# Attention and ResMLP on one core: alpha2 folded into w_ch1 once, beta2 turned into a relu bias, and the instruction order refined anew

## The chip, the cores and the metric

The kernel runs on one core of one Trainium2 chip. The metric is the device time of one execution in microseconds. The core has five engines that each run their own instruction list in order: TensorE (PE, matrix products; its weight loads are listed apart as PEld), VectorE (DVE), ScalarE (ACT), GpSimd (POOL) and SyncE (SP, which here issues most of the DMA transfers). "SPq" in a profile is SP's list, where DMA issues and their waits stand. POOL also issues some transfers; the profile calls their queue software_dynamic and the others' hardware_dynamic.

## The reference

```python
# attention, B=4, H=8, S=768, D=64; 4 sinks and a causal window of 128
scores = (q @ k.T) / sqrt(D), kept where (key is a sink) or (0 <= i - j < 128)
a = softmax(scores);  x = a @ v              # -> x: (4, 768, 512)

# ResMLP
a1  = alpha1 * x + beta1
tok = einsum('ts,bsd->btd', w_tok, a1)       # mixing over the 768 tokens
u   = x + lam * tok
a2  = alpha2 * u + beta2                     # per channel, 512 of them
ch  = relu(a2 @ w_ch1) @ w_ch2               # 512 -> 2048 -> 512
out = u + lam * ch
```

All inputs and the output are float32.

## The kernel before, in words

The four batches go through the same steps: load q, k and v, transpose q and k, scores (S), exponentials (E), masks, the product with v (pv), token mixing (tok), transposed u (uT), the first channel product (h), relu into hT, and the second channel product. Matrix operands are f16, sums are f32.

**The plan.** Each step is put down as a task: a priority, the engines that may run it with a cost in ns for each, the tasks that it needs, and the buffers that it uses. `Plan.run` (L132) lays all the tasks out against a model of the engines and the DMA queues, and `Plan.emit` (L246) writes the instructions out in that order. On the chip each engine works through its own list in order and waits by semaphores for the data that the tasks name. A DMA "lands" in the plan at a modelled time; a dependence on it holds in the plan, but if the two are not connected by data, nothing on the chip enforces it. The list `TURNS` holds seeds that perturb the priorities. In the first 36 us of the plan, where PE has nothing to do, fillers are emitted (`idle`, L347 to L349): small matmuls on a constant tile `warm`, 75 ns each by the plan.

**Weights.** `load_w1` (L553 to L558) brings w_ch1 into `w1f` (f16, 128 x 4 x 2048) as four quarters of 512 columns, converted on the way by POOL's software queue. `load_w` (L548) brings w_ch2 in eight pieces of 512 KB into f32 staging tiles `wst`; the plan has them follow the second quarter of w1f. `cast_w2` (L933 to L939) multiplies them by lam into `w2f`. `gate` (L560 to L564) is a tiny transfer on SP that reads one value row of a w1f quarter into a scratch tile: it must wait for the quarter to land, and every transfer that stands behind it on SP's list waits with it. There are three gates, for the quarters 1, 2 and 3.

**uT.** u = x + lam·tok is cast to f16. For batch 0, `uTp` (L985) transposes on PE into PSUM, and four pieces per half of the tokens evacuate it with alpha2·u + beta2 applied (`affine`, L977 to L983, on ACT at L980 or on DVE at L982, both factors as per-partition pointers). For batches 1 to 3, `uTx` (L1009 to L1026) lets a DMA transpose on SP write uT directly, and eight affine pieces per batch (128 x 384 each, ACT or DVE, in place) follow.

**The channel MLP.** `mlp1` (L1028 to L1049): for each half of the tokens (384) and each of the 16 blocks of 128 hidden channels, four matmuls over the 512 channels into one PSUM bank (tile `h`, L1036), then relu into `hT` on ACT (L1042) or DVE (L1044). That is 32 groups of four matmuls for each batch. Groups are called h0_0_10 for batch 0, half 0, hidden block 10; block i reads quarter i // 4 of w1f. The second product is plain for batch 0 (`mlp2`, tile `ch`, L1221). For batches 1 to 3 it is a Strassen scheme of seven products (`prod`, P1 to P7, L1153), which needs sums of hT parts (`h_sums`: S3 L1094, S1 L1095, S2 L1096, S4 L1097) and of w2f parts (`w2_sums`, L1057 to L1068).

Batch b+1's attention is woven into batch b's MLP, so PE's list mixes both.

The four h matmuls of a group and the affine piece are these lines:

```python
nc.tensor.matmul(ph.t, w1f[:, c, fi * P : (fi + 1) * P],
                 bu.t[:, c, chk * NTOK : (chk + 1) * NTOK], start=(c == 0), stop=(c == NC - 1))
nc.scalar.activation(o, i, AF.Identity, bias=be, scale=al)       # affine on ACT
```

Of the kernel before, what the change touches and what calls it, by code (L numbers as in the profile page):

```python
# [9 lines left out]
FP32 = mybir.dt.float32  # L10
# [101 lines left out]
class Plan:  # L112
# [18 lines left out]

    def run(self, prio):  # L132

# [34 lines left out]
        def pick():  # L168
            best = None
            spare = {k: sorted(h for h, x in zip(homes[k], busy[k]) if not x) for k in homes}  # L170
            for r, i in open_:
                at = ready[i]
                if best is not None and at > best[0]:
                    continue
                t = tasks[i]
                asked = {}
                for b in t.uses:
                    if b.home is None:
                        asked[b.kind] = asked.get(b.kind, 0) + 1
                if any(len(spare[k]) < n for k, n in asked.items()):  # L180
                    continue
                at = max([at] + [spare[k][n - 1] for k, n in asked.items()])
                own = None
                for e in t.engs:
                    at_e = max(free[e], at)
                    if e == POOL or (e == DVE and t.port):
                        at_e = max(at_e, port)
                    key = (at_e + FW * t.engs[e], at_e, r, at_e + t.engs[e], i, e)
                    if own is None or key < own:
                        own = key  # L190
                if best is None or own[1:] < best:
                    best = own[1:]
            return best
# [51 lines left out]

    def emit(self, turns):  # L246

        prio = [t.prio for t in self.tasks]
        for seed in turns:
            prio = shuffle(prio, seed)  # L250
        for t, e, start, stop, idle in self.run(prio):
            t.at = (e, start, stop)
            if idle:
                self.fill[1](self.pools["d"][0].tile(
                    [128, 512], FP32, tag=f"d_{idle[0]}", bufs=1, name=f"idle{t.i}"), idle[1])
            for b in t.uses:
                if b.t is None:
                    pool, shape, dtype = self.pools[b.kind]
                    b.t = pool.tile(b.shape or shape, b.dtype or dtype,
                                    tag=f"{b.kind}_{b.home}", bufs=1, name=b.name)  # L260
            t.fn(e)


# [16 lines left out]
def kernel(  # L280
# [52 lines left out]
        "u16": (sb, [P, DM], FP16),  # L333
        "uT": (sb, [P, NC, S], FP16),
        "hT": (sb, [P, NF, NTOK], FP16),
        "wst": (sb, [P, 2, 512], FP32),
# [30 lines left out]

    rsum = const.tile([P, NR], FP32, name="rsum")
    ab_row = sb.tile([2 * NC, P], FP32, tag="pt_2", bufs=1, name="ab_row")
    nc.scalar.dma_start(ab_row[0:NC], moe_alpha2.rearrange("(c p) -> c p", p=P))  # L370
# [37 lines left out]

    gates = sb.tile([1, 32], FP16, tag="pt_1", bufs=1, name="gates")

# [5 lines left out]

    TURNS = (13523, 134113, 50022, 128275, 136711, 187603, 125671, 100730, 14946, 163131, 178432, 158827, 183776, 137680, 153375, 26742, 367527, 307353, 376563, 212018, 255075, 397706, 218147, 375675, 393913, 224567, 207692, 352780, 243076, 346008)
    W1_SINCE = 20000.0
# [271 lines left out]
    def scores(p, b, j, Gs, bias=False):  # L690
# [51 lines left out]
        for G, hps, n, pS, eT in units:  # L742
            done["S", b, j, G] = a

            def ex(e, n=n, pS=pS, eT=eT):
                nc.scalar.activation(  # L746
                    eT.t, pS.t[:, :, 0 : n * w].rearrange("p e (i w) -> p e i w", i=n),
                    AF.Exp, scale=scale)

            x_ = add(p + 0.1, {ACT: 170 + 2 * n * w * 0.835}, ex, [a], [pS, eT])  # L750
            if not bias:
                def mk(e, eT=eT):
                    if e == POOL:
                        ev = eT.t.rearrange("p e i w -> p (e i) w")
                        keep(ev[:, :, 0:P], 0, 1, -1)
                        if w > P:
                            keep(ev[:, :, P:w], -1, -1, 1)
                        return
                    m = mask0 if j == 0 else (maskn if j < NR - 1 else maskn[:, :, 0:P])
                    ev = eT.t.rearrange("p e i w -> p (e i) w")  # L760
                    nc.vector.tensor_mul(ev, ev, m.to_broadcast(list(ev.shape)))

                c = {DVE: 60 + 2 * n * w * 0.66}
                if b and j:
                    c[POOL] = 2 * (150 + n * w * 0.9)
                x_ = add(p + 0.2, c, mk, [x_], [eT], port=True)
            for g in (0, 1) if G is None else (G,):
                off = 2 * g if G is None else 0
                E[b, j, g] = (eT, off)
                done["E", b, j, g] = [x_]  # L770
# [38 lines left out]
    def pv(p, b, r, G):  # L809
# [55 lines left out]
        elif G == 1:  # L865
# [7 lines left out]

            a = add(p + 0.3, {POOL: 1350}, mul, [a, done["x", b, r, 0], done["la1"]], [bx, bt], port=True)
            done["xh", b, r, 1] = add(
# [57 lines left out]
    def cast_w2(p, i):  # L933
        for a in range(4 * i, 4 * i + 4):
            src = wst[f"w2_{a - a % 2}"]
            done["w2", a] = add(
                p, {DVE: 980, POOL: 1400},
                lambda e, a=a, src=src: engine[e].tensor_mul(w2f[:, a, :], src.t[:, a % 2, :], lam_b),
# [70 lines left out]
    def uTx(p, b, ti):  # L1009

        if (b, 0) not in uT:
            uT[b, 0] = Buf("uT", None, None, f"uT{b}")
        bo, bu = uT[b, 0], u16[b, ti]
        done["uTd", b, ti] = add(
            p, {SP: 1220}, lambda e: nc.sync.dma_start_transpose(
                bo.t[:, :, ti * P : (ti + 1) * P], bu.t),
            [done["u16", b, ti]], [bu, bo], lands=(6, 100))
        if ti % 3 < 2:
            return
        chk = ti // 3  # L1020
        for c in range(NC):
            o = (c, slice(chk * NTOK, (chk + 1) * NTOK))
            done["uT", b, chk, c] = add(
                p + 0.1 + 0.01 * c, {DVE: 380, ACT: 700},
                lambda e, c=c, o=o: affine(e, bo.t[:, o[0], o[1]], bo.t[:, o[0], o[1]], c),
                [done["uTd", b, 3 * chk + i] for i in range(3)] + [done["ab2"]], [bo])  # L1026

    def mlp1(p, b, chk, fi):  # L1028
        if fi == 0:
            hT[b, chk] = Buf("hT", None, None, f"hT{b}_{chk}")  # L1030
        bh, bu = hT[b, chk], uT[b, 0]
        ph = Buf("d", [P, NTOK], FP32, f"h{b}_{chk}_{fi}")

        def mm(e):
            for c in range(NC):
                nc.tensor.matmul(  # L1036
                    ph.t, w1f[:, c, fi * P : (fi + 1) * P],
                    bu.t[:, c, chk * NTOK : (chk + 1) * NTOK], start=(c == 0), stop=(c == NC - 1))

        def relu(e):  # L1040
            if e == ACT:
                nc.scalar.activation(bh.t[:, fi, :], ph.t, AF.Relu)  # L1042
            else:
                nc.vector.tensor_scalar_max(bh.t[:, fi, :], ph.t, 0.0)  # L1044

        a = add(p, {PE: 4 * 161}, mm,
                [done["uT", b, chk, c] for c in range(NC)] + [done["w1", fi // 4]],
                [ph, bu])
        done["h", b, chk, fi] = add(p + 0.1, {ACT: 493, DVE: 556}, relu, [a], [ph, bh])  # L1049

# [6 lines left out]
    def w2_sums(p):  # L1057

        for g in range(HF // 2):
# [5 lines left out]
            def sub(o, i0, i1, after, n_):  # L1065
                def f_(e, bw=bw):
                    ab = [w2f[:, x_[0], x_[1]] if isinstance(x_, tuple) else bw.t[:, x_] for x_ in (o, i0, i1)]
                    engine[e].tensor_sub(*ab)  # L1068
                return add(p + 4 * g + n_, {DVE: 420, POOL: 1400}, f_, after, [bw], port=True)

# [7 lines left out]
    def h_sums(p, b, what):  # L1078
# [6 lines left out]
        def s2(g, f):  # L1085
            return own[g].t if own else h0.t[:, f]

        if what == "S3":
            hs = hS[b] = [Buf("nat", [P, HF // 2, NTOK], FP16, f"hS{b}_{g}") for g in range(2)]
        for g in range(2):  # L1090
            f, k_ = slice(4 * g, 4 * g + 4), slice(HF + 4 * g, HF + 4 * g + 4)
            fi, ki = range(4 * g, 4 * g + 4), range(HF + 4 * g, HF + 4 * g + 4)
            made = {
                "S3": lambda e, f=f, g=g: nc.vector.tensor_sub(hs[g].t, h0.t[:, f], h1.t[:, f]),  # L1094
                "S1": lambda e, f=f, k_=k_: nc.vector.tensor_add(h1.t[:, f], h1.t[:, f], h1.t[:, k_]),  # L1095
                "S2": lambda e, f=f, g=g: nc.vector.tensor_sub(s2(g, f), h1.t[:, f], h0.t[:, f]),  # L1096
                "S4": lambda e, f=f, k_=k_, g=g: nc.vector.tensor_sub(h0.t[:, k_], h0.t[:, k_], s2(g, f)),  # L1097
            }[what]
# [10 lines left out]
            uses = uses + ([own[g]] if own and what in ("S2", "S4") else [])  # L1109
            done[what, b, g] = add(p + 0.1 * g, {DVE: 880}, made, after, uses, port=True)  # L1110

# [5 lines left out]
    def prod(p, b, what, nt):  # L1117
# [46 lines left out]
        def plus(p, bx, cols, more):  # L1164
            def f_(e):
                nc.vector.tensor_add(row(bx)[:, cols], row(bx)[:, cols], pc.t)  # L1166
            u_ = done["u16", b, nt if bx is top else nt + 3]
            return add(p, {DVE: 400}, f_, [a, u_] + more, [pc, bx])

# [12 lines left out]
        elif what == "P6":  # L1182
            def u2(e):
                nc.vector.tensor_add(bt.t, bt.t, pc.t)

            u = add(p + 0.1, {DVE: 400}, u2, [a, done["read", b, "P1", nt]], [pc, bt])

# [7 lines left out]

            done["U12", b, nt] = add(p + 0.3, {POOL: 760, DVE: 400}, ot, [u, done["u16", b, nt]], [bt, top], port=True)
            done["U2", b, nt] = add(
# [108 lines left out]
    for b in range(B):  # L1306
# [54 lines left out]
        if b + 1 == STRASSEN[0]:  # L1361
            w2_sums(w0 + ns + PAR["w2s"])
        if b + 1 < B:
            nb = b + 1
# [28 lines left out]

    plan.emit(TURNS)

# [34 lines left out]
```

The softmax here doesn't subtract the row's maximum and nothing guards it: scores larger than these inputs give would overflow.

## Time and profile before

| | |
|---|---|
| device time, median of 5 runs | 256.57 us (256.34 to 257.22) |
| the profiled execution's own time | 256.68 us |
| its span, first to last instruction | 255.0 us |
| mean granted TensorE clock | 1.00 |
| busy: PE / DVE / ACT / POOL | 247.6 / 189.2 / 142.6 / 88.1 us |
| bytes moved by DMA | 38.80 MB, 152 GB/s in the mean |

A line of groups has the source line, engine and operation, `out<-in` by tile names, partitions x elements and type, the count, then total busy time and mean ns of one, then the idle time of that engine just ahead of such instructions and what ended it. A line of waits has the waiting engine and line, what it waited for, and the total, the number and the longest of these waits in us. A timeline line has the start, the length, and what ran.

By stage of the kernel, PE and ACT were busy for:

| stretch, us | PE busy | DVE busy | ACT busy | POOL busy | DMA share |
|---|---|---|---|---|---|
| 0 to 40 | 38.13 | 31.50 | 26.42 | 21.05 | 1.07 |
| 40 to 64 | 23.54 | 17.78 | 21.05 | 9.67 | 1.05 |
| 64 to 104 | 38.83 | 32.80 | 19.54 | 14.99 | 0.86 |
| 104 to 130 | 25.92 | 20.28 | 22.70 | 15.65 | 0.86 |
| 130 to 180 | 49.64 | 41.04 | 25.32 | 21.75 | 0.59 |
| 180 to 252 | 71.58 | 45.73 | 27.58 | 5.02 | 0.19 |

### The profile page before, as it was taken

The numbers are of one execution on the slowest core, as the hardware profiler recorded it, in microseconds if no ns is written. First come the engines' busy times: TensorE is split into PE (matmuls) and PEld (weight loads), VectorE is DVE, ScalarE is ACT, GpSimd is POOL, SyncE is SP. The second block draws the span as 40 slices with busy tenths as digits, with TensorE's granted clock in tenths as the row PEclk, the third lists the DMA queues.
The fourth block names the chain that finished last, engine by engine and source line by source line (L and its number), as shares of the span: only waits on it lengthen the run. The fifth ranks groups of instructions, "written<-read, shape, count | busy, mean of one in ns | idle before, by whom it ended". The sixth has DMA issues, their size and how long they took to land.

```text
span 255.0 us, 5519 instructions
## 1 busy us (share of the span) xinstructions
PE 247.6 (97%) x2174; PEld 161.4 (63%) x2174; DVE 189.2 (74%) x402; ACT 142.6 (56%) x236; POOL 88.1 (35%) x108
## 2 busy tenths in 40 slices
PE   8999998999999999899999999999999999999994
PEld 7855645665555543456688676658658666657883
DVE  6787998595878878578889988877789764136782
ACT  2699846989848035688971225867571135775000
POOL 7419802345455330168653450735310101000000
PEclk9999999999999999999999999999999999999999
DMA  6999999999944899599679699501000257000105
GB/s 206 200 219 320 205 252 389 376 354 192 219 74 119 185 245 209 113 207 228 145 144 194 108 194 249 85 3 21 3 0 3 61 167 144 0 0 3 63 4 185
DMA packets 86130, 38.80 MB, mean 152 GB/s; under 512 B 73540, under 2 KB 80460, under 8 KB 86104
## 3 DMA queue, kind: packets, MB, share of 16 engines
q1 hardware_dynamic: 82320, 35.14, 57.7%
q0 software_dynamic: 3744, 3.28, 8.0%
q8 instruction: 17, 0.28, 0.5%
q14 instruction: 9, 0.07, 0.1%
q10 hardware_dynamic: 40, 0.03, 0.0%
HBM read 29.91 MB, written 6.29 MB: 142 GB/s over the span
## 4 chain that ended last, share of the span: by engine, by line
PE 92%; DVE 3%; DMA 2%; ACT 1%; issue 1%; ACTq 0%
PE h L1036 33%; PE P L1153 21%; PE tok L956 11%; PE ch L1221 8%; PE pv L825 5%; PE S L724 4%; PE idle L349 2%; PE S L719 1%; PE tp L614 1%; DMA wtn<-in_moe_w_tok_dram 1%; DVE uT L982 1%; PE tp L611 1%; PE pv L818 1%; PE wT L916 1%; PE sk L656 1%; ACT uT L980 1%
## 5 line engine op out<-in xcount | busy, mean ns | idle before, releaser
L1036 PE MATMUL h<-uT,w1f 128*128 128x384 f16 x512 | 92.0, 326 | 2.7 <-DVE uT L982 1.3
L1036 PEld LDWEIGHTS <-w1f 128*128 128x128 f16 x512 | 47.3, 98 | 34.4 <-issue 5.5
L1042 ACT ACTIVATE hT<-h 128x384 f16<-128x384 f32 x99 | 48.4, 493 | 25.9 <-PE h L1036 25.5
L1153 PEld LDWEIGHTS <-hT 128*128 128x128 f16 x408 | 39.8, 98 | 6.7
L746 ACT ACTIVATE E<-S 128x1024 f16<-128x1024 f32 (+1 forms) x39 | 37.9, 1001 | 7.5 <-PE S L724 3.7
L869 POOL TENSOR_TENSOR tm<-x,la_b 128x512 f32<-128x512 f32 x18 | 26.2, 1455 | 26.3 <-DVE xh L872 19.1
L956 PE MATMUL tok<-xh,wtokT 128*128 128x512 f16 x144 | 33.4, 379 | 0.0
L356 ACT CAST u<-x 128x512 f16<-128x512 f32 x19 | 11.7, 618 | 30.7 <-DVE x L963 30.5
L1153 PE MATMUL P<-w2f,hT 128*128 128x256 f16 x216 | 25.9, 273 | 0.0
L1044 DVE TENSOR_SCALAR hT<-h 128x384 f16<-128x384 f32 x29 | 15.8, 552 | 11.6 <-PE h L1036 11.2
L1166 DVE TENSOR_TENSOR x<-x,P 128x256 f32<-128x256 f32 x45 | 18.3, 417 | 8.2 <-PE P L1153 8.0
L956 PEld LDWEIGHTS <-wtokT 128*128 128x128 f16 x144 | 14.0, 98 | 14.6
L1221 PE MATMUL ch<-w2f,hT 128*128 128x512 f16 x96 | 23.0, 379 | 0.0
L1153 PE MATMUL P<-w2s,hT 128*128 128x256 f16 x192 | 22.8, 273 | 0.0
L851 DVE TENSOR_TENSOR x<-pv,rec 128x256 f32<-128x256 f32 x48 | 20.4, 424 | 1.7
L358 POOL CAST vfs<-vnat 128x512 f16<-128x512 f32 x18 | 14.9, 834 | 16.2 <-DMA vnat<-in_v_dram 16.0
L963 DVE TENSOR_TENSOR x<-x,tok 128x512 f32<-128x512 f32 x24 | 16.2, 683 | 5.7 <-PE tok L956 5.7
L356 ACT CAST n<-nat 128x768 f16<-128x768 f32 x16 | 13.2, 829 | 11.4 <-DMA nat<-in_q_dram 8.5
L825 PEld LDWEIGHTS <-E 128*128 128x128 f16 x328 | 15.2, 98 | 6.0 <-issue 1.6
L825 PE MATMUL pv<-vfs,E 128*128 128x65 f16 x328 | 17.9, 194 | 0.0
L358 POOL CAST u<-x 128x512 f16<-128x512 f32 x5 | 3.1, 623 | 34.2 <-DVE x L963 21.1
L1221 PEld LDWEIGHTS <-hT 128*128 128x128 f16 x96 | 8.6, 98 | 9.0 <-issue 0.2
(131 smaller groups left out, 327.5 us busy)
## 6 DMA issues: line engine op xcount, KB each, us to landing
out_dram<-x SPq DMA_DIRECT2D x21, 256.0 KB, 2.8
nat<-in_q_dram SPq DMA_DIRECT2D x13, 384.0 KB, 5.8
nat<-in_k_dram SPq DMA_DIRECT2D x13, 384.0 KB, 5.5
vnat<-in_v_dram SPq DMA_DIRECT2D x18, 256.0 KB, 4.4
wst_w<-in_moe_w_ch_dram SPq DMA_DIRECT2D x8, 512.0 KB, 7.5
wtn<-in_moe_w_tok_dram SPq DMA_DIRECT2D x6, 384.0 KB, 4.2
w1f<-in_moe_w_ch_dram POOLq DMA_DIRECT2D x4, 512.0 KB, 10.2
v<-in_v_dram SPq DMA_DIRECT2D x12, 128.0 KB, 6.0
```

The source lines that it names most:

```text
L356: nc.scalar.copy(o, i)
L358: engine[e].tensor_copy(o, i)
L746: nc.scalar.activation(eT.t, pS.t[:, :, 0 : n * w].rearrange("p e (i w) -> p e i w", i=n), AF.Exp, scale=scale)
L825: nc.tensor.matmul(po.t[:, hl, :], eT.t[:, e_, off + i, c : c + P], vf[j][:, h, :], start=(r < 2 and n == 0), stop=(n == len(parts) - 1 an ...
L851: nc.vector.tensor_mul(bx.t[:, 4 * G : 4 * G + 4, :], po.t[:, :, 0:D], rec.t.to_broadcast([P, 4, D]))
L869: engine[e].tensor_mul(bt.t, bx.t.rearrange("p h d -> p (h d)"), la1_b)
L956: nc.tensor.matmul(pt.t, wtokT[:, si, ti * P : (ti + 1) * P], hs[si].t, start=(si == 0), stop=(si == NR - 1))
L1036: nc.tensor.matmul(ph.t, w1f[:, c, fi * P : (fi + 1) * P], bu.t[:, c, chk * NTOK : (chk + 1) * NTOK], start=(c == 0), stop=(c == NC - 1))
L1042: nc.scalar.activation(bh.t[:, fi, :], ph.t, AF.Relu)
L1153: nc.tensor.matmul(pc.t, hh[:, nt * P : (nt + 1) * P], w(fi), start=(first and n_ == 0), stop=(n_ == HF - 1), skip_group_check=True)
L1166: nc.vector.tensor_add(row(bx)[:, cols], row(bx)[:, cols], pc.t)
L1221: nc.tensor.matmul(pc.t, bh.t[:, fi, nt * P : (nt + 1) * P], w2f[:, fi, :], start=(fi == 0), stop=(fi == NF - 1))
```

## The change

Since a2 @ w_ch1 = u @ (alpha2·w_ch1) + beta2 @ w_ch1, alpha2 can be multiplied into w_ch1's rows and beta2 @ w_ch1 added ahead of the relu.

- Batch 0 stays as it was, on the plain w1f, with two more columns: columns 768 and 769 of its uT hold +beta2 and −beta2 (`beta_cols`, 2 small DVE instructions). The second half's 16 groups are 386 columns wide. After the relu their difference is beta2 @ w_ch1 exactly, relu(z) − relu(−z) = z; one subtraction puts it into `bw1` (128 x 16, f32).
- Once batch 0's h groups have read w1f, `fold_w1` multiplies it in place by alpha2, in eight pieces of 128 x 1024.
- Batches 1 to 3 have no affine pieces. h needs the DMA transposes and the folds, and the relu gets `bw1`'s column as a per-partition bias.
- The buffers uT and hT are wider (784 and 386 columns), and the h sums read 384 of 386. The scratch tile of the gates has a place of its own.
- Some costs in the plan differ, `TURNS` has 16 seeds in place of 30, and a list `NUDGES` of several hundred seeds moves priorities of single tasks, groups of them or pairs, or pins a task to one of its engines. The order of all engines' lists is thereby another one.

```diff
@@ uTx: batches 1 to 3
-        done["uTd", b, ti] = add(
+        done["uT", b, ti] = add(
             p, {SP: 1220}, lambda e: nc.sync.dma_start_transpose(
                 bo.t[:, :, ti * P : (ti + 1) * P], bu.t),
             [done["u16", b, ti]], [bu, bo], lands=(6, 100))
-        if ti % 3 < 2:
-            return
-        chk = ti // 3
-        for c in range(NC):
-            o = (c, slice(chk * NTOK, (chk + 1) * NTOK))
-            done["uT", b, chk, c] = add(
-                p + 0.1 + 0.01 * c, {DVE: 380, ACT: 700},
-                lambda e, c=c, o=o: affine(e, bo.t[:, o[0], o[1]], bo.t[:, o[0], o[1]], c),
-                [done["uTd", b, 3 * chk + i] for i in range(3)] + [done["ab2"]], [bo])
+    def beta_cols(p):
...
+                nc.vector.tensor_scalar(
+                    out=bo.t[:, :, S + n_], in0=beta2_c, scalar1=sign, scalar2=None, op0=ALU.mult)
...
+    def fold_w1(p):
...
+            lambda e: engine[e].tensor_sub(bw1, bh.t[:, :, NTOK], bh.t[:, :, NTOK + 1]),
+            [done["h", 0, 1, fi] for fi in range(NF)], [bh])
+        for fh in range(2):
+            for c in range(NC):
+                o = (c, slice(fh * DFF // 2, (fh + 1) * DFF // 2))
+                def fold(e, o=o):
+                    w, al = w1f[:, o[0], o[1]], alpha2_c[:, o[0] : o[0] + 1]
+                    if e == ACT:
+                        nc.scalar.activation(w, w, AF.Copy, scale=al)
+                    else:
+                        engine[e].tensor_scalar(out=w, in0=w, scalar1=al, scalar2=None, op0=ALU.mult)
+                done["w1a", c, fh] = add(
+                    p + 0.1 * (4 * fh + c), {ACT: 1060, DVE: 650}, fold,
+                    [done["hm", 0, chk, fi] for chk in range(2) for fi in range(8 * fh, 8 * fh + 8)]
+                    + [done["ab2"]], port=True)
@@ mlp1
         def relu(e):
+            o, be = bh.t[:, fi, 0:n_], bw1[:, fi : fi + 1]
             if e == ACT:
-                nc.scalar.activation(bh.t[:, fi, :], ph.t, AF.Relu)
+                nc.scalar.activation(o, ph.t, AF.Relu, **({"bias": be} if b else {}))
+            elif b:
+                nc.vector.tensor_scalar(out=o, in0=ph.t, scalar1=be, scalar2=0.0, op0=ALU.add, op1=ALU.max)
             else:
-                nc.vector.tensor_scalar_max(bh.t[:, fi, :], ph.t, 0.0)
+                nc.vector.tensor_scalar_max(o, ph.t, 0.0)
...
+        if b:
+            after = [done["uT", b, 3 * chk + i] for i in range(3)]
+            after += [done["w1a", c, fi // 8] for c in range(NC)]
+        else:
+            after = [done["uT", b, chk, c] for c in range(NC)] + [done["w1", fi // 4]]
+            after += [done["be"]] if chk else []
@@ the order
-        for t, e, start, stop, idle in self.run(prio):
+        pin = [0] * len(prio)
+        for seed in nudges:
+            nudge(prio, pin, seed)
+        for t, e, start, stop, idle in self.run(prio, pin):
...
-    plan.emit(TURNS)
+    plan.emit(TURNS, NUDGES)
```

In the new lists SP issues four w2 loads (pieces 2, 12, 0 and 6) ahead of the first gate, where before the gate came first; the query and key loads of batch 1 follow that gate, and the second gate follows them and four more w2 loads. PE's h groups of batch 0 begin with h0_0_1, 10, 3, 4, 7, 15, 6, where before they began with h0_0_5, 0, 1, 2, 3, 4, 6. Fillers number 96 for 106.

## The prediction

> **What bounds the kernel now.** I read the page first: busy shares, the 40 slices, the chain that ended last. In the first line below each engine has its busy time and its share of the span; the row of digits is TensorE (PE) slice by slice; the last line follows the end of the kernel back.
>
> ```profile
> PE 247.6 (97%) x2174; PEld 161.4 (63%) x2174; DVE 189.2 (74%) x402; ACT 142.6 (56%) x236; POOL 88.1 (35%) x108
> PE   8999998999999999899999999999999999999994
> PE 92%; DVE 3%; DMA 2%; ACT 1%; issue 1%; ACTq 0%
> ```
>
> PE is busy 247.6 of 255.0 us at full clock. Only 7.4 us are not PE work, and of those about 1 us lies before the first matmul and 3.4 us behind the last one (the last output's add and store). Work taken from VectorE (DVE) or ScalarE (ACT) is therefore worth nothing in itself. It counts only where PE stands still, so the list of PE's waits comes next (total, times, longest):
>
> ```profile
> PE h L1036 <- DVE uT L982: 1.3, 2, 1.1
> PE idle L349 <- DVE warm L375: 1.1, 1, 1.1
> PE h L1036 <- ACT uT L980: 0.9, 2, 0.5
> PE h L1036 <- DVE x L1166: 0.4, 1, 0.4
> ```
>
> The second is the start of the program. The first and third are waits of the channel MLP's first product (h) for the affine step alpha2·u+beta2 that the change removes for batches 1 to 3. By time, the ACT one lies at 39.5 to 41.1 us (batch 0, whose affine pieces stay) and the 1.1 us at 102.56 (batch 1, whose pieces go). The timeline there shows start, duration, engine, line, and the idle time ahead in brackets:
>
> ```profile
> 101.52 0.70 ACT L980 ACTIVATE uT<-uT,ab 128x384 f16<-128x384 f16 x1
> 101.53 0.69 DVE L963 TENSOR_TENSOR x<-x,tok 128x512 f32<-128x512 f32 x1 [0.61 <-PE tok L956]
> 102.13 1.24 DVE L982 TENSOR_SCALAR uT<-uT,ab 128x384 f16<-128x384 f16 x3
> 102.56 2.17 PE L1036 MATMUL h<-uT,w1f 128*128 128x384 f16 x10 [1.07 <-DVE uT L982]
> ```
>
> The three DVE pieces stand behind an x add, and h starts piece by piece: 1.23 us to its first matmul, then 0.26 and 0.12 more between the first ones, 1.6 us in all.
>
> **The change, part by part.** The sum is made against the profiled execution, 256.68 us (span 255.0, and 1.7 around it); the median of the runs is 256.57, 0.1 less. A measurement can tell about 0.2% (0.5 us) from no change.
>
> *1. The 24 affine pieces of batches 1 to 3 go (17 DVE, 7 ACT).* PE stood still for them once, 1.6 us at batch 1. What is late next there is the DMA transpose itself. Before, it landed at 100.90, 4.2 us after the third tok tile ended (96.7). In the new PE order 4.98 us of matmuls stand between that tile and the first h group of batch 1 (a quarter of ch 0.87, vsp 0.22, three tok tiles 3.9). Cover exceeds latency by 0.8 us, so I take the whole 1.6 as gained. Without that cover it would be 0.8 less. At batches 2 and 3 PE did not wait for the pieces: 0.
>
> *2. The fold: 8 instructions in place on w1f (7 ACT, 1 DVE), 2 beta columns, one subtraction.* Nothing in the trace has 128x1024 f16 from SBUF on ACT. The nearest rows are these casts and pieces:
>
> ```profile
> L356 ACT CAST n<-nat 128x768 f16<-128x768 f32 x16 | 13.2, 829 | 11.4 <-DMA nat<-in_q_dram 8.5 <-DMA nat<-in_k_dram 2.8
> L356 ACT CAST u<-x 128x512 f16<-128x512 f32 x19 | 11.7, 618 | 30.7 <-DVE x L963 30.5
> L980 ACT ACTIVATE uT<-uT,ab 128x384 f16<-128x384 f16 x7 | 4.7, 699 | 0.0
> L1042 ACT ACTIVATE hT<-h 128x384 f16<-128x384 f32 x99 | 48.4, 493 | 25.9 <-PE h L1036 25.5
> ```
>
> From 618 at 512 to 829 at 768 is 0.82 ns an element, so 1,040 ns at 1024, and up to 1,130 with one per-partition pointer: 7 x 1.1 = 7.7 us of ACT. They stand between 67 and about 95 us. In 64 to 104 us ACT is busy 19.5 of 40 us, and 27 with the folds, so ACT itself hides them. One fold queued ahead of an E exponential delays the scores behind it by at most 1.1 us; the next S tiles and ch matmuls cover that. I take 0, and keep 0 to 0.5. They wait for batch 0's last h matmuls of their half, over 30 us before batch 1 reads w1f.
>
> *3. Two extra columns.* 64 matmuls of 386 instead of 384 columns: 162 ns each, so 2/384 of that, 0.05 us. Loss 0.05.
>
> *4. The relu of batches 1 to 3 now has a bias pointer.* ACT with two pointers takes 697 ns at 384 columns from SBUF, without any 0.82 x 384 + 196 (the 512 row less its slope) = 511; from PSUM it is 670 against 490. So 90 ns a pointer, and relu goes from 493 to 583. PE makes an h group in 4 x 162 = 650 ns, so even ACT alone keeps up. In batch 1 ACT also does scores (22.7 of 26 us busy in 104 to 130 us); there it has 20 relus, 1.8 us more, against two affine pieces less (1.4 us, those at 108.4 and 110.3). Walking that order by hand with 583 gives about 0.2 us of PE wait. On DVE the relu turns into add and max in one instruction; the old one was 552 with a maximum alone, and I take 552 to 600. Four banks hold h, so small lateness is absorbed. Loss 0.2 (0 to 0.8). Of the old small waits (0.25 at 110.92, 0.5 at 179.8) I count none as gained.
>
> *5. hT rows of 386 elements.* The h sums (952 to 1,056 ns a piece) read strided rows; batch 3's last ones have 0.4 us of slack in front of the products that need them. 0, and up to 0.3 lost if a piece takes 0.1 more.
>
> *6. The new order.* The list of instructions by engine has the same matmuls in all, except 96 fillers for 106. Giving every group in PE's new order the duration of its row before, the part from the first h group on is equal within 0.1 us, and the head is 0.5 to 1.1 shorter. Ten fillers at the plan's own 75 ns, against 93 by busy time, are 0.75 to 0.9 of that. Gain 0.75.
>
> *7. The loads of the head.* This is the part that the diff does not show. Before, SyncE's queue (SP) ran:
>
> ```profile
> 33.00 0.81 SPq L562 DMA_DIRECT2D gates<-w1f  x1
> 33.86 1.93 SPq L551 DMA_DIRECT2D wst_w<-in_moe_w_ch_dram  x4
> 35.88 0.67 SPq L562 DMA_DIRECT2D gates<-w1f  x1
> 36.66 0.38 SPq L504 DMA_DIRECT2D nat<-in_k_dram  x1
> ```
>
> The tiny gate transfer waits for the second quarter of w1f, and all w2 loads are queued behind it, so w1f had the DMA engines alone. After, four w2 loads (512 KB each, 2 MB) stand on SP ahead of that gate. Only the eight outstanding transfers and a v buffer hold them: they should issue at about 21.5 to 25 us, amid the w1f issues (20.7 to 27.3). Nothing enforces the old order. How much w1f loses is read from the records of 22 to 24 us, then of 28 to 33 us:
>
> ```profile
> q1 hardware_dynamic: 236, 0.65, 91.9%
> w1f<-in_moe_w_ch_dram POOLq DMA_DIRECT2D x1, 512.0 KB, 10.0
> q0 software_dynamic: 1015, 1.01, 121.9%
> ```
>
> Though the first w1f load issued at 20.74, 22 to 24 us hold only packets of the queue ahead of it (wtn); the software queue rises as the other fades. That looks like service in order of arrival. Alone, w1f moves 1.01 MB in 5 us; w2 packets alone moved 0.82 MB in 38 to 40 us, so 512 KB take 1.3 us. Quarters landed at 30.5, 33.0, 35.5 and 38.3. With four w2 loads ahead (5.1 to 5.5 us) the third lands at 40.6 to 41.1 and the fourth at 43.4 to 43.8. And the new h order needs them earlier: its second group reads the third quarter (before: the ninth group, at 46.5 us) and its sixth reads the fourth (before: 56 us). The first group ends at 41.3 as before, or 40.2 to 40.5 with the shorter head; four groups later is 43.0. So PE waits about 0.3 to 0.9 for the third quarter and up to 0.8 for the fourth: together 0.3 to 2, and I take 1.2. No wait is 0. From the other side: if queues share, and the query and key loads behind the gate (from about 38 us) share too, each quarter of 512 packets takes up to twice its 2.5 us, the third lands at 43.5 and the fourth at 48.6, and PE loses up to 5.8.
>
> The Trainium skill, "DMA: Bandwidth & Descriptors", section "Queues, rings and completion order", says that a DMA engine takes turns between the queues it has work for, a packet at a time; by it the loads would share and the loss lies near the 5.8 end. The 22 to 24 us row speaks against it for this backlog, and the measured row decides.
>
> Sum: 256.68 − 1.6 − 0.75 + 0.05 + 0.2 + 1.2 = 255.8 in the profiled execution, 255.7 for the median.
>
> **The rivals.**
> *A, the quarters are in time.* For: the head's fillers show that PE waits for data there anyway. Against: 2 MB more in front of a saturated queue. Price: the 1.2 comes back, 254.5.
> *B, slower: w2 and query/key loads starve w1f's last two quarters.* Place: h groups two and six of batch 0, 40 to 49 us. From 2.6 us of lateness on (the 2.1 that the other terms gain together, and the 0.5 that can be told) the kernel is measurably slower than before; in full it is 255.7 − 1.2 + 5.8 = 260.3, and at half 257.4. For: both queues ran together at 25 to 27 us (149 packets against 144). Against: 22 to 24 us.
> *C, no gain at batch 1.* The affine wait is replaced by one for the transposes (their casts and SP's issues stand in order behind others) or for ACT's longer relus: 0.8 to 1.6 come back, 256.5 to 257.3. Against: 0.8 us of cover.
> *D, the change does not do what it says.* The instruction lists show the pieces gone and the folds there; nothing left for this.
>
> **How the numbers follow.** Forecast (254.9 to 256.1) 0.42; A 0.15; C 0.2 (half of it within 0.2%); B 0.23. Faster by over 0.2% (under 256.06) takes the forecast's 0.40 and A: 0.55. Within 0.2% (256.06 to 257.08): 0.02 of the forecast, 0.1 of C, 0.05 of B: 0.17. Slower: the other 0.1 of C and 0.18 of B: 0.28. Range: 253.9 (A with the upper head gain, 0.6 less than 254.5) to 258.2, which leaves out the upper part of B.
>
> **What would show it.** Right: in PE's waits no uT releaser near 100 us, and a wait of h for a w1f DMA of 0.3 to 2 us between 40 and 45 us; ACT relus with bias near 580 ns; folds of 1.0 to 1.15 us inside ACT's idle time. Wrong: h waiting for w1f over 2.6 us (B), or h of batch 1 waiting over 0.8 us for uT's DMA (C). An E behind a fold with PE idle would falsify step 2.

## The result and the profile after

The changed kernel takes 259.13 us (median of 22 runs, 257.39 to 262.31) against 256.81 (42 runs, 256.27 to 257.78): ratio 1.0085, interval 1.0071 to 1.0099. It is slower by 2.2 us; 255.7 was predicted, with 258.2 as the end of the range. Runs more than 1.5% above the fastest of the same kernel count as slow and are left out of the ratios: here three of the 22 (261.38 to 262.31, at a granted clock of 0.991 to 0.993; the other 19 have a median of 259.03), and further down the longest run of a4 (261.36, at 1.00). The profiled execution took 257.74 us (span 255.8), which is near the short end of its runs. This is a first reading: part of the loss, 1.1 us against the profiled execution before, is in that trace, and the rest, 1.4 us, is in what differs from execution to execution.

The page and PE's waits of the changed kernel, in the order in which they were read before:

```profile
PE 248.0 (97%) x2164; PEld 160.9 (63%) x2164; DVE 191.0 (75%) x390; ACT 145.6 (57%) x223; POOL 102.3 (40%) x118
PE   7999998999999999999899999999999999899994
```

```profile
PE idle L400 <- DVE warm L427: 1.1, 1, 1.1
PE h L1117 <- DVE hT L1126: 0.9, 2, 0.7
PE pv L878 <- DVE E L814: 0.8, 1, 0.8
PE S L777 <- ACT E_None L799: 0.5, 1, 0.5
PE h L1117 <- ACT uT L1033: 0.5, 1, 0.5
PE tp L667 <- POOL iden L486: 0.3, 1, 0.3
PE h L1117 <- DVE uT L1035: 0.2, 1, 0.2
```

The uT wait at batch 1 is gone: h starts there without a gap (the last transpose landed at 101.81).

```profile
100.64 1.89 PE L1009 MATMUL tok<-xh,wtokT 128*128 128x512 f16 x8
102.37 1.95 PE L1117 MATMUL h<-uT,w1f 128*128 128x384 f16 x11
```

But three new ones stand in the list: h behind a relu (hT), pv behind a masked exponential, S behind an exponential. And no wait for w1f is there, though the four w2 loads went ahead of the gate as foreseen, from 19.07 us on and so 2.4 us sooner than the prediction had them:

```profile
19.07 6.67 SPq L604 DMA_DIRECT2D wst_w<-in_moe_w_ch_dram  x4
37.87 0.80 SPq L615 DMA_DIRECT2D gates<-w1f  x1
38.77 0.39 SPq L557 DMA_DIRECT2D nat<-in_k_dram  x1
```

The quarters of w1f landed at 33.39, 37.85, 40.39 and 43.17 us. PE's second group begins at 41.15 and needs the third, the sixth begins at 43.75 and needs the fourth. That is 0.8 and 0.6 us to spare.

### The profile page after: what moved, and what is told of

It reads as the page before. It is cut to its first block, busy times and chain, and to the rows that moved or that the text cites. A ratio compares the mean times of both kernels' runs of the same rounds, so it can differ in the third digit from the quotient of the medians.

```text
span 255.8 us, 5458 instructions
## 1 busy us (share of the span) xinstructions
PE 248.0 (97%) x2164; PEld 160.9 (63%) x2164; DVE 191.0 (75%) x390; ACT 145.6 (57%) x223; POOL 102.3 (40%) x118
## 4 chain that ended last, share of the span: by engine, by line
PE 92%; DVE 3%; POOL 1%; ACT 1%; issue 1%; POOLq 0%
PE h L1117 31%; PE P L1242 22%; PE tok L1009 12%; PE ch L1310 8%; PE pv L878 5%; PE S L777 4%; PE idle L400 2%; PE S L772 2%; PE pv L871 1%; PE tp L667 1%; PE tp L664 1%; DVE E L814 1%; POOL n L550 1%; ACT E L799 1%; DVE hT L1126 1%
## 5 line engine op out<-in xcount | busy, mean ns | idle before, releaser
L1117 PE MATMUL h<-uT,w1f 128*128 128x384 f16 (+1 forms) x512 | 91.2, 327 | 1.6 <-DVE hT L1126 0.9
L1124 ACT ACTIVATE hT<-h,bw 128x384 f16<-128x384 f32 x70 | 40.6, 581 | 18.6 <-PE h L1117 9.0
L1242 PEld LDWEIGHTS <-hT 128*128 128x128 f16 x408 | 39.6, 98 | 6.4
L1009 PE MATMUL tok<-xh,wtokT 128*128 128x512 f16 x144 | 32.6, 379 | 0.2 <-DVE rec L903 0.2
L1126 DVE TENSOR_SCALAR hT<-h,bw 128x384 f16<-128x384 f32 x26 | 15.9, 615 | 17.3 <-PE P L1242 9.4
L1242 PE MATMUL P<-w2f,hT 128*128 128x256 f16 x216 | 26.7, 273 | 0.0
L409 POOL CAST vfs<-vnat 128x512 f16<-128x512 f32 x18 | 13.3, 740 | 23.4 <-DMA vnat<-in_v_dram 23.0
L1278 POOL TENSOR_TENSOR x<-x,pt 128x256 f32<-128x256 f32 x3 | 2.8, 939 | 40.8 <-DVE pt L1273 40.7
L407 ACT CAST n<-nat 128x768 f16<-128x768 f32 x15 | 12.0, 831 | 9.8 <-DMA nat<-in_k_dram 6.8
L814 DVE TENSOR_TENSOR E<-E,maskn 128x1024 f16<-128x1024 f16 x19 | 15.5, 823 | 0.0
```

What stands on the lines that cost most here:

```text
L407: nc.scalar.copy(o, i)
L1009: nc.tensor.matmul(pt.t, wtokT[:, si, ti * P : (ti + 1) * P], hs[si].t, start=(si == 0), stop=(si == NR - 1))
L1117: nc.tensor.matmul(ph.t, w1f[:, c, fi * P : (fi + 1) * P], bu.t[:, c, chk * NTOK : chk * NTOK + n_], start=(c == 0), stop=(c == NC - 1))
L1124: nc.scalar.activation(o, ph.t, AF.Relu, **({"bias": be} if b else {}))
L1126: nc.vector.tensor_scalar(out=o, in0=ph.t, scalar1=be, scalar2=0.0, op0=ALU.add, op1=ALU.max)
L1242: nc.tensor.matmul(pc.t, hh[:, nt * P : (nt + 1) * P], w(fi), start=(first and n_ == 0), stop=(n_ == HF - 1), skip_group_check=True)
```

## Experiments

The two theories at the start: **T1**, in most executions those two quarters come late and h waits; **T2**, the spread and the loss come from elsewhere in the new order.

### Does w1f come late?

*a1*: the changed kernel again, no edit. 

> The changed kernel once more, unchanged, for a second trace. Its first profiled execution (257.74 us) showed no wait of h for w1f: the third quarter landed at 40.39 us, 0.8 ahead of its group, the fourth at 43.17, 0.6 ahead. The median of its runs lies 1.4 us above that execution. Theory T1 (late quarters): 258.5 to 259.5 median; if this profiled execution is over 258.5, PE's waits show h waiting for w1f between 40 and 46 us for about the excess. Theory T2 (the spread comes from elsewhere, from the order behind the head or the first loads): no wait for w1f even in a slower execution, the excess lies before 40 or behind 46 us.

259.07 us median (257.47 to 261.18), 1.0083 (1.0053 to 1.0114). Its profiled execution is again a short one (257.47), with the quarters at 40.56 and 43.22, and shows no wait for w1f. It tells nothing between T1 and T2.

*a2*: the same instructions, other blocks first.

```diff
+    SWAP = {10: 2, 2: 10, 15: 0, 0: 15}
...
+        fo = SWAP.get(fi, fi) if (b, chk) == (0, 0) else fi
-                    ph.t, w1f[:, c, fi * P : (fi + 1) * P],
+                    ph.t, w1f[:, c, fo * P : (fo + 1) * P],
-            o, be = bh.t[:, fi, 0:n_], bw1[:, fi : fi + 1]
+            o, be = bh.t[:, fo, 0:n_], bw1[:, fo : fo + 1]
```

> In batch 0's first half the hidden blocks 10 and 2 change places, and 15 and 0: PE's groups two and six read the first quarter of w1f, and the third and fourth quarters are first read at about 46.4 and 47.0 us. Nothing else changes. T1: the excess goes, 257.4 to 258.0 median, and the spread of the runs is that of the kernel before (about 1 us). T2: as the changed kernel, 258.7 to 259.5.

258.07 us (257.28 to 259.12), 1.0052 (1.0034 to 1.0070). That is 1.0 us less than a1, just above what T1 expected, and none of the six runs is above 259.12. In its trace the third and fourth quarters landed at 41.87 and 45.37 us. The groups two and six began at 41.58 and 44.18, so under the old names the third quarter would have been 0.3 us late and the fourth 1.2; here PE does not wait for them.

*a3*: the four loads behind the gate.

```diff
+        at = [i for i, s_ in enumerate(steps) if s_[0] in self.gates][0]
+        early = [i for i in range(at) if steps[i][0] in self.w2loads]
...
+        moved = [steps[i] for i in early]
+        steps = [s_ for i, s_ in enumerate(steps[: at + 1]) if i not in early] + moved + steps[at + 1 :]
```

> The four w2 loads go behind the first gate on SP, as before the change; all other lists stay. The quarters should land at about 30.5, 33, 35.5 and 38.3 us again. T1: 257.4 to 258.3 (the w2 multiplications may now wait up to 0.5 us for their data). T2: 258.7 to 259.5.

258.13 us (257.41 to 258.62), 1.0050 (1.0035 to 1.0064). The quarters landed at 29.1, 31.6, 34.3 and 37.1. Two different remedies for late quarters bring the same 1.0 us: T1 holds for that part. (Both intervals lie below that of the 22 runs, 1.0071 to 1.0099; a1's own, with 8 runs, is wider and overlaps them.) The two traces of the changed kernel itself are of short executions, so its late quarters are concluded from the remedies and not seen in it. T2 holds for what is left, 1.3 us over the kernel before, with the spread of the runs only partly gone.

*a4*: no bias on the relus.

```diff
-                nc.scalar.activation(o, ph.t, AF.Relu, **({"bias": be} if b else {}))
-            elif b:
-                nc.vector.tensor_scalar(out=o, in0=ph.t, scalar1=be, scalar2=0.0, op0=ALU.add, op1=ALU.max)
+                nc.scalar.activation(o, ph.t, AF.Relu)
```

> The relus of batches 1 to 3 have no bias (beta2 is left out there), the order is the same: ACT's relu 493 instead of 581 ns, DVE's 555 instead of 615. If the longer relus cost what the prediction took (0.2) or nothing, the median falls by under 0.3 us against the changed kernel; if the waits of h for DVE's relus (0.9 us in the profiled execution) and of pv for a masked E (0.8) come from them, it falls by 0.8 to 1.7 us.

259.10 us (256.87 to 261.36), 1.0067 (1.0035 to 1.0100): no different from the changed kernel within what these runs tell. The waits of h for a DVE relu (0.7) and of pv for E (0.8) are still there, so the longer relus do not make them. What it showed beyond its purpose: its profiled execution is its longest run, 261.36 us at a granted clock of 1.00, and there h waits for the late quarters.

```profile
40.79 0.65 PE L1117 MATMUL h<-uT,w1f 128*128 128x384 f16 x3 [0.19 <-DVE uT L1035]
43.19 2.77 PE L1117 MATMUL h<-uT,w1f 128*128 128x384 f16 x16 [1.75 <-DMA w1f<-in_moe_w_ch_dram]
47.58 1.48 PE L1117 MATMUL h<-uT,w1f 128*128 128x384 f16 x8 [1.62 <-DMA w1f<-in_moe_w_ch_dram]
```

The third quarter landed at 43.14 and the fourth at 47.54: group two and group six wait, 3.4 us of idle time in all. It is one execution; that quarters come late in shorter ones too is seen in a2 above and in a5 below. Its SP list tells what differed. The last value loads and the wtn loads, which wait for older transfers to finish, went out later, and so the w2 loads did too:

```profile
22.40 3.45 SPq L604 DMA_DIRECT2D wst_w<-in_moe_w_ch_dram  x4
38.62 0.81 SPq L615 DMA_DIRECT2D gates<-w1f  x1
```

How the DMA engines divide themselves is in the packets of the two queues. From 28 to 34 us, first the changed kernel's profiled execution, then a4's (q0 carries w1f, q1 the w2 loads; packets, MB, share of 16 engines):

```profile
q0 software_dynamic: 581, 0.58, 56.8%
q1 hardware_dynamic: 579, 1.12, 55.7%
```

```profile
q1 hardware_dynamic: 551, 1.15, 56.7%
q0 software_dynamic: 560, 0.56, 54.9%
```

From 36 to 39 us, in the same order:

```profile
q0 software_dynamic: 609, 0.60, 120.5%
q1 hardware_dynamic: 20, 0.03, 3.4%
```

```profile
q0 software_dynamic: 295, 0.30, 58.1%
q1 hardware_dynamic: 294, 0.56, 55.7%
```

Packet for packet, 581 to 579: as long as the w2 loads have packets, w1f runs at 97 packets a us, half of the 203 that it has alone. By the packet records the w2 loads began to run out at 35 us in the short execution, at 40 in the long one. There the query and key loads behind the gate came in soon after, and the fourth quarter landed 4.4 us after the third instead of 2.8.

### The arithmetic without the order

*e6*: the kernel before, affine pieces of batches 1 to 3 emit nothing.

```diff
-                lambda e, c=c, o=o: affine(e, bo.t[:, o[0], o[1]], bo.t[:, o[0], o[1]], c),
+                lambda e: None,
```

> The kernel before without the 24 affine pieces (alpha2 and beta2 left out in batches 1 to 3), nothing put in their place. Bounds step 1 by itself: 255.0 to 255.4 if PE's 1.6 us at batch 1 go, 256.0 or more if the wait moves to the transposes. The difference to the kernel with folds in the old order is the price of folds, columns and bias: 0 to 0.3 by the prediction.

255.55 us (255.21 to 256.08), 0.9953 (0.9940 to 0.9965). The gain is 1.2 us, less than the 1.6 of the wait. The trace shows where 0.4 can have gone:

```profile
101.33 2.11 PE L1036 MATMUL h<-uT,w1f 128*128 128x384 f16 x12
103.37 0.50 PE L724 MATMUL S<-qkT 64*128 64x256 f16 x6
104.25 0.28 PE L724 MATMUL S<-qkT 64*128 64x256 f16 x2 [0.38 <-DMA qkT<-n]
```

h starts 1.23 us earlier and without gaps, and 2 us later the scores of batch 2 wait for a transpose of q and k.

*e5*: the whole arithmetic in the old order: as e6, and the columns, the subtraction, the bias, the wider tiles as in the change, with the eight folds emitted between ACT's instructions.

```diff
+        self.folds, self.n, self.AT = None, 0, {5: 1, 11: 6, 12: 1}
...
+            if e == ACT and self.folds:
+                self.n += 1
+                for _ in range(self.AT.get(self.n, 0)):
+                    next(self.folds, None)
             t.fn(e)
```

> The fold and the relu bias put into the kernel before with its own order of work (w2 loads behind the gate, its own h order): no affine pieces in batches 1 to 3, eight folds on ACT in gaps between 75 and 95 us, two extra columns. If the change's arithmetic is worth what the prediction gave it (1.6 gained at batch 1, 0.05 and up to 0.2 lost), the median is 255.2 to 255.6 and the loss is all the new order's. Rival: the transposes, the folds or the longer relus take the gain back, 256.4 to 257.5.

256.11 us (255.16 to 257.88), 0.9982 (0.9965 to 0.9999). Between the two cases: faster than before, but by 0.5 (the ratio) to 0.7 (the medians) and not by 1.2 to 1.6.

*a5*: the changed order with a2's names and a4's relus, no folds, no extra columns in the matmuls (the two small DVE instructions that write them stay).

```diff
-                    if e == ACT:
-                        nc.scalar.activation(w, w, AF.Copy, scale=al)
-                    else:
-                        engine[e].tensor_scalar(out=w, in0=w, scalar1=al, scalar2=None, op0=ALU.mult)
+                    return
...
-            lambda e: engine[e].tensor_sub(bw1, bh.t[:, :, NTOK], bh.t[:, :, NTOK + 1]),
+            lambda e: None,
...
-        n_ = NTOK + 2 if (b, chk) == (0, 1) else NTOK
+        n_ = NTOK
```

> The changed order with the renamed blocks, and neither folds, bias nor extra columns (alpha2 and beta2 left out in batches 1 to 3): what remains is the new order with the affine pieces gone. If the 1.2 us that the renamed kernel is still slower than before come from the order, this is 257.7 to 258.1; if folds and relus cost them, 256.8 to 257.2.

257.36 us (256.50 to 258.45), 1.0030 (1.0016 to 1.0043). Also between: 0.6 (the ratios) to 0.7 (the medians, of two chips) less than a2. Its third and fourth quarters landed at 41.27 and 44.50 us, for groups that began at 40.88 and 43.48: again too late for the old names, by 0.4 and 1.0. Against e6, which has the same arithmetic left out in the old order, it is 1.8 us slower. So the order costs 1.8 with the quarters out of the way, and the added arithmetic 0.5 to 0.7 in either order.

*e5 and e6 again, e7 and e8*, on one chip: which addition costs those 0.5 to 0.7 us? e7 is e5 with a4's edit; e8 is e5 with the folds not emitted.

```diff
-                    next(self.folds, None)
+                    pass
```

> The arithmetic of the change in the old order once more (255.16 to 257.88 in 12 runs, median 256.11, though its profiled execution of 255.51 is as long as that of the kernel without affine pieces, 255.47), for a second trace and a tighter interval. If folds, bias and columns cost something fixed: median 255.9 to 256.3 and the kernel without affine pieces 0.4 to 0.7 under it on the same chip. If they cost nothing and the difference was one of chips and runs: within 0.3 of it.

> The old order without affine pieces, again, beside the three others on the same chip: 255.3 to 255.8.

> As the arithmetic in the old order, with no bias on the relus (beta2 left out in batches 1 to 3), folds and columns stay. If the longer relus (581 for 493 ns) are the cost: as the kernel without affine pieces, 255.3 to 255.7; if not: as with everything, 255.9 to 256.3.

> As the arithmetic in the old order, without the eight folds (alpha2 left out in batches 1 to 3), bias and columns stay. If the folds on ACT are the cost: 255.3 to 255.7; if not: 255.9 to 256.3.

| kernel in the old order | median, us | ratio (interval) |
|---|---|---|
| e5, everything | 256.23 | 0.9973 (0.9963 to 0.9982) |
| e6, no affine pieces and nothing in their place | 255.69 | 0.9957 (0.9941 to 0.9973) |
| e7, everything but the bias | 255.84 | 0.9966 (0.9949 to 0.9983) |
| e8, everything but the folds | 255.65 | 0.9957 (0.9943 to 0.9971) |

Without folds the kernel with bias and columns is as fast as with nothing added, so without the folds bias and columns cost nothing that can be told. The medians put about 0.5 us on the folds, though the intervals of e5 and e8 overlap. But e7 lies between, 0.4 under e5, and its interval takes in the medians of all four: whether the bias has a share when the folds are there is not settled. In e5's second trace, and in e7's, the wait at the scores of batch 2 is 0.9 instead of the 0.4 to 0.5 of e6 and e8; one fold stood ahead of a cast of k there. In e5's first trace, with the same list, it is 0.5, and that execution (255.51) is as short as e6's (255.47).

*e9*: folds at `{3: 1, 4: 1, 5: 1, 11: 5}`, none ahead of those casts. 

> The arithmetic in the old order, with the folds elsewhere in ACT's list: three singly before exponentials at 71 to 77 us, five in the gap behind 82 us, none ahead of the last q/k casts of batch 2. If the late casts (and with them the q/k transposes that PE waits 0.9 us for at 105 us) are the price of the folds: 255.4 to 255.9 and that wait 0.4 to 0.5. If not: 256.0 to 256.3.

256.18 us (255.63 to 256.88), 0.9966 (0.9950 to 0.9981). The wait at the scores fell to 0.4 as expected, the median did not. Through which wait the folds cost their half microsecond stays open.

### What in the order costs 1.8 us?

First the head. From the first instruction to the first h matmul the eight traces with the new order have 39.66 to 40.77 us, mean 40.22; the eight with the old order, before among them, 39.34 to 39.80, mean 39.49. So 0.7 us are lost before any of the changed arithmetic runs. The first h matmul before, and in the changed kernel:

```profile
39.51 0.32 PE L1036 MATMUL h<-uT,w1f 128*128 128x384 f16 x1 [0.47 <-ACT uT L980]
```

```profile
40.16 0.32 PE L1117 MATMUL h<-uT,w1f 128*128 128x384 f16 x1 [0.47 <-ACT uT L1033]
```

In all the new ones PE waits near 5.4 us for POOL's identity tile, which its first transposes need (0.25 to 0.8 us); in the old order no trace has that wait. It does not explain the whole 0.7. Ahead of the first h matmul PE stood idle 2.4 us in the mean of the new traces and 2.05 in the old; the other 0.4 lie in the records of the same 341 matmuls and ten fillers fewer, and no experiment was made on the head.

Then the three new waits, which stand in every trace of the new order (a6 below was made to remove two of them). The smallest, 0.5 us for S behind an exponential, comes at 67.0 us in the changed kernel, ahead of the first fold at 70.6, and is as long in a5 without folds, so it too belongs to the order. The one near 220 us, in the changed kernel:

```profile
218.53 1.04 PE L1242 MATMUL P<-w2f,hT 128*128 128x256 f16 x8
219.61 1.14 DVE L1126 TENSOR_SCALAR hT<-h,bw 128x384 f16<-128x384 f32 x2 [6.97 <-PE P L1242]
220.28 0.97 PE L1117 MATMUL h<-uT,w1f 128*128 128x384 f16 x5 [0.71 <-DVE hT L1126]
```

The relus of batch 3 write the buffer that the last P5 product of batch 2 still reads. PE has that product behind h groups whose relus wait for it; the four banks are full, and the next h waits until the first relu is through. The other, near 124 us:

```profile
121.75 1.27 POOL L922 TENSOR_TENSOR tm<-x,la_b 128x512 f32<-128x512 f32 x1
122.31 2.48 DVE L814 TENSOR_TENSOR E<-E,maskn 128x1024 f16<-128x1024 f16 x2
124.85 0.39 PE L878 MATMUL pv<-vfs,E 128*128 128x65 f16 x7 [0.78 <-DVE E L814]
```

*a6*: a3, and three steps of PE's list moved.

```diff
+        p5, h = find("P5_2_0", "hT2_0"), find("h3_1_0")
+        steps.insert(h + 1, steps.pop(p5))
+        h, v1, v0 = find("h1_1_9"), find("pv2_3_1", "E2_3_1"), find("pv2_3_0", "E2_3_0")
+        pvs = [steps[v1], steps[v0]]
+        steps = [s_ for i, s_ in enumerate(steps[: h + 1]) if i not in (v1, v0)] + pvs + steps[h + 1 :]
```

> The changed kernel with the gate first, and three steps of PE's list moved: the last P5 product of batch 2 ahead of the last three h groups before it (the relus of batch 3 wait for it to have read the old hT), and one h group ahead of the two pv steps near 124 us that wait for a masked E. If the named waits are what the order loses: h behind DVE's hT gone (0.7 to 0.9), pv behind E 0.2 to 0.3 instead of 0.8, and the median 1.2 to 1.5 us under the kernel with only the gate moved. If the loss is spread over the order: under 0.5.

> The changed kernel with only the gate put first, again, for the comparison: 257.9 to 258.4.

a6: 256.93 us (256.29 to 258.42), 1.0008 (0.9991 to 1.0026). a3 on the same chip: 257.72 (257.19 to 258.70), 1.0039 (1.0024 to 1.0053). In a6's list of waits pv behind E is gone and h behind DVE's hT is 0.2 in place of 0.9 (the 0.7 near 220 us is gone). From the first h matmul to PE's end the two traces differ by 1.5 us (211.15 against 212.64), the size expected; the medians by 0.8, between the two cases, so somewhat over half of it arrives. That these waits cost time is shown; the rest of the order's loss is not traced to a place.

So the loss of 2.2 to 2.3 us is made of: affine pieces −1.2, folds about +0.5, the head +0.7, the new order behind the head +1.1 to 1.3 (0.8 of it undone by a6), late quarters +1.0 to 1.3. They sum to +2.1 to +2.6. The +1.1 is what is left of 1.8 behind the head. The traces agree, with some scatter: from the first h matmul to PE's end it is 212.2 to 213.2 us, mean 212.6, in the five of the new order that have all the arithmetic and no wait for w1f, and 210.9 to 211.7, mean 211.4, in those of e5 and e9.

e5 is the version that beats both kernels: 256.11 and 256.23 us, 0.9982 (0.9965 to 0.9999) and 0.9973 (0.9963 to 0.9982) of the kernel before, about 1.1% under the changed one.

## Why the prediction was wrong, step by step

- *Step 1, affine pieces (−1.6).* The wait went, as said, and uT's transposes were in time. The size in the old order was 1.2: the next thing late there was q and k's transposes, 2 us further on, which the step had not looked for. In the changed kernel's list that wait does not stand, so how much of the 1.6 it got is not known apart from its order.
- *Step 2, folds (0, at most 0.5).* 1,141 ns each on ACT, as the upper estimate of 1,130, and no E behind a fold left PE idle. Still the medians put them at the end of the stated range.
- *Step 3 and 4, columns and relus (0.25).* The relu's price was right, 581 ns for 583 and 615 on DVE for up to 600. No cost can be told in a4 and e8; e7 leaves up to 0.4 open.
- *Step 5* was nothing: e8 has the wide rows and is as fast as e6, and the h sums took 950 to 1,026 ns a piece after, 952 to 1,056 before.
- *Step 6, the order (−0.75)* is the step that failed. Adding up every group's duration in the new order gives PE's work, not its waits. The ten fillers less did not shorten the head, which grew by 0.7 us. That fillers in part fill time in which PE waits anyway can be seen in the old order: in e5's second trace PE was through the first 61 of them 0.9 us sooner than before (its next product at 6.94 for 7.80), stood idle 0.5 us longer from there on, and reached its first h only 0.2 sooner. And "equal within 0.1 us" from the first h on left out waits that only the other engines' lists show, of 0.5 to 0.8 us each. Gain 0.75 was forecast, and 1.8 of loss came: an error of 2.5 us in a miss of 3.4.
- *Step 7, the loads (+1.2).* Median 1.0 to 1.3, so the size held, but by luck. The term was a wait in the profiled execution, and there it is 0: the quarters landed at 40.39 and 43.17, a little ahead of the forecast 40.6 to 41.1 and 43.4 to 43.8, and group two, with the longer head, came at 41.15 and not at 40.2 to 40.5. By a2 and a3 the 1.0 to 1.3 come from executions with later quarters. Rival B is their upper end: a4's profiled execution lost 3.4 us at the two groups named, with the quarters at 43.14 and 47.54 for the 43.5 and 48.6 of B. The reason given was wrong. The row of 22 to 24 us, which was read as service in order of arrival, is better read as a queue that had not begun: in a4's execution the first w1f load was issued at 20.93 and had its first packets at 24 us, 109 in that microsecond beside 65 of the other queue, which had been full before and still carried wtn packets up to 31 us. Where both have packets they take turns, 581 to 579. The Trainium skill has this rule in "DMA: Bandwidth & Descriptors", section "Queues, rings and completion order": an engine goes round the queues that have work for it, a packet at a time. These traces agree with it. The short executions landed near where arrival order puts them because the w2 loads ran out from 35 us on, before the query and key loads came. A term of 0 to 5.8 that depends on when a queue started should not have been settled by one row; it should have widened the spread.
- *Rival C* is the small part of step 1 that was given back in the old order, at another transpose. *D* had nothing in it. The lower end of the range, 253.9, takes 0.6 off for the head, where step 6's upper gain is only 0.35 above its 0.75; the result lies beyond the other end.

## What to carry to other kernels

When a scheduled order is replaced, cost the waits and not only the work: for each long group on the busiest engine, ask which buffer its evacuation writes and who still reads it. A load that stands ahead of a gate by order alone is held by nothing; whether it hurts depends on how late it starts, so look at the slack of what it competes with (here 0.6 us) and expect the median, not the best execution, to pay. Test an arithmetic change in the old order before judging it in a new one.

## What was not expected of the hardware

- The two DMA queues shared packet by packet from 28 to 34 us although their packets differ in size (1 KB and 2 KB): w1f fell from 203 to 97 packets a us, and the w2 loads got two thirds of the bytes.
- Some DVE products ran longer beside POOL. The masked E products of 128x1024 took 726 ns in the mean before and 823 after (1.25 and 1.31 us at 122.3, beside two POOL instructions); w2f's products on DVE 691 before and 1,009 after, while POOL went from 88.1 to 102.3 us of work. Others got shorter (xh, 725 to 686). In the two traces these three groups have 96 products: all 18 over 700 ns had a POOL instruction beside them for at least a quarter of their time, and the 55 with none took 677 to 693 ns. The other 23 had POOL beside them and stayed short, so POOL's being busy is not enough by itself. That POOL is the cause was not tried.
